# Splitting three of layer two's output-weight pairs earlier, in a two-layer gated network after channel attention

## The chip, the cores and the metric

One core of one Trainium2 chip runs the kernel. The metric is the device time of one execution in microseconds. Three runs of the kernel before took 1188.28, 1188.49 and 1191.84 us; the median is 1188.49.

## The reference

Channel attention over 6016 tokens and 256 channels gives x; two gated layers with 1536 hidden features follow, the first with an RMS norm and silu, the second with a sigmoid:

```python
def _attn_ref(q, k, v, tau):
    qn = q / (np.linalg.norm(q, axis=1, keepdims=True) + 1e-06)
    kn = k / (np.linalg.norm(k, axis=1, keepdims=True) + 1e-06)
    s = kn.transpose(0, 2, 1) @ qn / tau
    a = np.exp(s - s.max(-1, keepdims=True))
    a /= a.sum(-1, keepdims=True) + 1e-09
    return v @ a

def _moe_ref(x, w_gate, w_val, w_out, rms_g):
    rms = np.sqrt(np.mean(x * x, axis=-1, keepdims=True) + 1e-06)
    xn = x / rms * rms_g
    g = xn @ w_gate
    silu = g * (1.0 / (1.0 + np.exp(-g)))
    return silu * (xn @ w_val) @ w_out

def _moe2_ref(x, w_gate, w_val, w_out):
    gate = 1.0 / (1.0 + np.exp(-(x @ w_gate)))
    return gate * (x @ w_val) @ w_out
```

## The kernel before

Every float32 matrix product is made from three matmuls: each operand is split into a high part (a copy on ACT that rounds to float32r) and a low part (a subtraction on DVE), and high x high, high x low and low x high are added up in PSUM (`mm3`, lines 107 to 109). On top of that, pairs of token blocks are multiplied by Strassen's scheme in Winograd's form, with seven products in place of eight.

The order of the work is written out by hand (`manual_schedule`); each engine takes its instructions in that order and stops at the first that has to wait. After the attention and some plain blocks of layer one, the program runs through *periods*. A period takes one of the 12 feature tiles f of one pair of token blocks p through the gate and value products.
- **The old-way block** (`period`, line 731): 12 periods, pair 2 of layer one. The gate and value products have seven factors, the output product is the ordinary one. A period is 33 matmul calls of 448 columns on PE, and 6.68 us long when nothing disturbs it.
- **The joint passes** (`team_period`, line 802): nine passes of 12 periods, three for layer one and six for layer two. Here the output product too has seven factors: six hidden tiles make a team of three pairs, and the team's 21 output products run in the six periods that follow. Accumulating transfers on POOL's queue (line 592) form the sums of hidden tiles.

Between two steps of a period there are named points (`early`, `ACT`, `DVE`, `end`) at which a list of callables is run: `slots[k][point]` belongs to the k-th of the periods still to come.

The joint passes need the *output weights* (w_out) in pairs of feature tiles, split into seven or eight pieces. Each layer has six such pairs. The split of one pair goes in two halves, from the rd buffers in DRAM into the od buffers:
- `out_load` (line 539) loads the four unsplit 128x128 pieces into tile t (256 KB).
- First half: `out_high` (line 547) copies t to its high part h on ACT; `out_low` (line 550) subtracts to the low part on DVE; each is stored to od by one transfer of 256 KB (line 554). `out_sums` (lines 558 to 561) then makes the four Winograd sums in t, on POOL.
- Second half: the same copy, subtraction and two stores, for the sums. It writes the same two tiles for the parts, so it has to wait until the first half's stores have landed.

Layer one's pairs use the tiles t1 to t3 of a pool with one buffer each; layer two's use three tiles of the `yo` ring, which the sums of the token pairs (line 407) use too. Pair i of layer one is split in the old-way block at the ends of periods 2i and 2i + 1. Pair 2u of layer two is split at the ends of periods 10 and 11 of joint pass u + 1, pair 2u + 1 at the ends of periods 0 and 1 of the pass after it. All loads and stores of this go through SP's queue, in the order written, together with the stores and loads of the input weights (gd, gw) and the loads of split output weights (ow, line 605). The input weights of feature tile f lie in the tiles wh`f` and wl`f`; the old-way block is the last to use them, and from there on the joint passes borrow these places.

Of the kernel before, what the change touches and what calls it, by code (L numbers as in the profile page):

```python
# [25 lines left out]
def kernel(  # L26
# [510 lines left out]
    odd = {}  # L537

    def out_load(l, i):
        if l:  # L540
            odd["t"], odd["h"], odd["l"] = (ip3.tile([P, 512], F32, tag="yo", name="o") for _ in range(3))
        else:
            odd["t"], odd["h"], odd["l"] = (sp.tile([P, 512], F32, tag=f"t{u}", name="o") for u in range(1, 4))
        nc.sync.dma_start(out=odd["t"], in_=rd[l][i].rearrange("p u n -> p (u n)"))

    def out_high(l, i):
        nc.scalar.copy(odd["h"].bitcast(F32R), odd["t"])

    def out_low(l, i, first):
        nc.vector.tensor_sub(odd["l"].bitcast(F32R), odd["t"], odd["h"])  # L550
        g, j = divmod(i, NJ)
        for e, t in enumerate((odd["h"], odd["l"])):
            dst = od[l][g][:, first : first + 4, e, j]
            nc.sync.dma_start(out=dst, in_=t.rearrange("p (u n) -> p u n", u=4))

    def out_sums(l, i):
        w11, w21, w12, w22 = (odd["t"][:, u * P : (u + 1) * P] for u in range(4))
# [42 lines left out]
    def ow_load():  # L600
        i, k = divmod(ow_n[0], len(KINDS))
        if i < len(teams):
            tag = ("wh3", "wl3", "wh4", "wl4")[ow_n[0] % 4]
# [299 lines left out]
    with tc.manual_schedule():  # L903
# [255 lines left out]

        def out_weights(l, i, one, two):  # L1160
            for slot, first in ((one, 0), (two, 4)):
                steps = [partial(out_high, l, i), partial(out_low, l, i, first)]
                slot.setdefault("end", []).extend(steps if first else [*steps, partial(out_sums, l, i)])
# [4 lines left out]

        out_load(0, 0)
        pv = None  # L1170
        outs = [(0, b // 2, b % 2, f) for b, f in items[-SKEW:]]
        for n, it in enumerate([*stream, None]):
# [17 lines left out]
            if n < NF and f % 2 == 0:  # L1190
                out_weights(0, f // 2, slots[0], slots[1])
                if f < NF - 2:
                    slots[1]["end"].append(partial(out_load, 0, f // 2 + 1))
            if 0 < n // NF < 4 and f == NF - 3:
                u = 2 * (n // NF - 1)
                slots[0].setdefault("end", []).append(partial(out_load, 1, u))
                out_weights(1, u, slots[1], slots[2])
                slots[2]["end"].append(partial(out_load, 1, u + 1))
            if 1 < n // NF < 5 and f == 0:
                out_weights(1, 2 * (n // NF - 1) - 1, slots[0], slots[1])  # L1200
# [9 lines left out]
            if pv and pv["it"][:2] == (0, PLAIN):  # L1210
# [3 lines left out]
                if g == 6:  # L1214
                    for _ in range(4):
                        ow_load()
# [43 lines left out]
```

## Time and profile before

| | us |
|---|---|
| median of three runs | 1188.49 (1188.28 to 1191.84) |
| the profiled execution | 1191.87 |
| its span, first to last instruction | 1190.1 |
| PE busy (matmuls) | 1156.2, 97% |
| DVE busy | 970.6, 82% |
| ACT busy | 889.9, 75% |
| POOL busy | 342.6, 29% |

PE is the matmul engine, DVE the vector engine, ACT the scalar engine, POOL the GpSimd engine, SP the engine that issues most transfers. All times in the rows are microseconds from the start of the span. A bracket at the end of a row tells how long the engine had been idle before it, and what ended that. In the names, o is any tile of the split above, hh and hl are the parts of a hidden tile, g and v PSUM banks. The old-way block runs from about 313 to 396 us, the joint passes from there to the end.

### The profile page before, as it was taken

How to read it: one execution, taken by the hardware profiler on the slowest of the kernel's cores; microseconds unless marked ns; L12 is line 12 of the kernel's file. 1: busy time of each engine (PE TensorE's matmuls, PEld its weight loads, DVE VectorE, ACT ScalarE, POOL GpSimd, SP SyncE). 2: the span in 40 equal slices, each digit the busy share in tenths (PEclk: the TensorE clock that was granted, in tenths of full speed). 3: DMA queues.
4: the chain of work that ended last, by engine and by line, in shares of the span. 5: the costliest groups of instructions: out<-in, count | busy, mean ns of one | idle time of the engine just before them, and what ended most of it. 6: DMA issues, size and time to landing. Idle time of an engine off the chain costs nothing.

```text
span 1190.1 us, 16698 instructions
## 1 busy us (share of the span) xinstructions
PE 1156.2 (97%) x5236; PEld 961.0 (81%) x5236; DVE 970.6 (82%) x1496; ACT 889.9 (75%) x1663; POOL 342.6 (29%) x399
## 2 busy tenths in 40 slices
PE   8899999999999999999999999999999999999997
PEld 7788788788899778788788778888888888888895
DVE  6798999986567588788898897887888888888877
ACT  6665778765577588787777877887787787787784
POOL 0042777742321122412412411321311321321121
PEclk9899999999999999999999999999999999999999
DMA  9663446774478879999999998998998998998995
GB/s 321 243 217 136 140 143 201 278 248 168 153 264 303 290 220 268 312 260 275 304 272 281 298 276 247 293 258 242 288 265 241 290 263 248 292 261 246 282 253 142
DMA packets 143000, 297.07 MB, mean 250 GB/s; under 512 B 13888, under 2 KB 53312, under 8 KB 142912
## 3 DMA queue, kind: packets, MB, share of 16 engines
q1 hardware_dynamic: 122032, 258.65, 64.3%
q0 software_dynamic: 20736, 37.23, 17.9%
q8 instruction: 41, 0.67, 0.2%
q14 instruction: 47, 0.39, 0.1%
q10 hardware_dynamic: 144, 0.13, 0.0%
HBM read 201.98 MB, written 56.75 MB: 217 GB/s over the span
## 4 chain that ended last, share of the span: by engine, by line
PE 67%; DMA 5%; DVE 3%; issue 3%; ACT 2%; POOL 0%; DVEq 0%; SPq 0%; ACTq 0%; POOLq 0%
PE g L107 10%; PE g L108 10%; PE g L109 10%; PE v L107 5%; PE v L109 5%; PE v L108 5%; PE y L108 4%; PE y L109 4%; PE y L107 4%; PE at L107 4%; PE at L108 4%; PE at L109 4%; DMA od<-o 3%; DMA hs<-hs 1%; DVE hl L648 1%
## 5 line engine op out<-in xcount | busy, mean ns | idle before, releaser
L592 POOL DMA_DIRECT2D hs<-hs x144 | 125.8, 926 | 572.2 <-DVE hl L648 416.3
L648 DVE TENSOR_TENSOR hl<-hs,hh 128x512 fp32r<-128x512 f32 (+1 forms) x324 | 223.8, 702 | 26.3 <-ACT hh L640 25.3
L640 ACT CAST hh<-hs 128x512 fp32r<-128x512 f32 (+1 forms) x324 | 195.0, 613 | 24.6 <-PE at L109 7.3
L833 ACT COPY v<-g 128x512 f32<-128x512 f32 (+1 forms) x210 | 119.0, 567 | 65.2 <-PE g L109 61.9
L838 DVE TENSOR_TENSOR hs<-g,e 128x512 f32<-128x512 f32 (+1 forms) x105 | 71.5, 681 | 67.4 <-ACT v L833 66.7
L107 PE MATMUL g<-xh,gw 128*128 128x512 f32 x240 | 95.0, 396 | 4.1 <-ACT v L833 2.8
L108 PE MATMUL g<-xl,gw 128*128 128x512 f32 x240 | 93.7, 391 | 0.0
L109 PE MATMUL g<-xh,gw 128*128 128x512 f32 x240 | 93.7, 390 | 0.0
L867 ACT ACTIVATE g<-g 128x512 f32<-128x512 f32 (+1 forms) x108 | 67.5, 625 | 29.8 <-DVE g L871 28.9
L108 PE MATMUL y<-hl,ow 128*128 128x512 f32 (+1 forms) x216 | 84.3, 390 | 1.8 <-DVE hl L648 1.7
L107 PE MATMUL y<-hh,ow 128*128 128x512 f32 (+1 forms) x216 | 84.2, 390 | 1.2 <-ACT hh L640 1.2
L109 PE MATMUL y<-hh,ow 128*128 128x512 f32 (+1 forms) x216 | 84.0, 389 | 0.0
L833 ACT COPY g<-g 128x512 f32<-128x512 f32 (+1 forms) x105 | 61.3, 583 | 25.4 <-PE g L109 25.0
L871 DVE TENSOR_TENSOR g<-g,g 128x512 f32<-128x512 f32 (+1 forms) x105 | 70.3, 670 | 5.6 <-PE g L109 5.6
L842 ACT ACTIVATE sg<-v 128x512 f32<-128x512 f32 (+1 forms) x108 | 64.2, 595 | 8.0 <-PE v L109 0.4
L107 PE MATMUL g<-qh,gw 128*128 128x512 f32 (+1 forms) x171 | 66.8, 390 | 2.9 <-ACT v L833 2.1
L108 PE MATMUL g<-ql,gw 128*128 128x512 f32 (+1 forms) x171 | 65.8, 385 | 0.0
L109 PE MATMUL g<-qh,gw 128*128 128x512 f32 (+1 forms) x171 | 65.7, 384 | 0.0
L108 PE MATMUL at<-hl,ow 128*128 128x512 f32 (+1 forms) x162 | 63.5, 392 | 0.5 <-DVE hl L648 0.4
L107 PE MATMUL at<-hh,ow 128*128 128x512 f32 (+1 forms) x162 | 63.2, 390 | 0.1
L109 PE MATMUL at<-hh,ow 128*128 128x512 f32 (+1 forms) x162 | 63.1, 389 | 0.0
L833 ACT COPY e<-g 128x512 f32<-128x512 f32 (+1 forms) x105 | 61.3, 583 | 0.4
(245 smaller groups left out, 3337.3 us busy)
## 6 DMA issues: line engine op xcount, KB each, us to landing
gw<-gd SPq DMA_DIRECT2D x216, 448.0 KB, 5.6
ow<-od SPq DMA_DIRECT2D x126, 384.0 KB, 5.2
hs<-hs POOLq DMA_DIRECT2D x128, 256.0 KB, 7.8
wraw<-in_w_dram SPq DMA_DIRECT2D x24, 768.0 KB, 4.7
od<-o SPq DMA_DIRECT2D x48, 256.0 KB, 4.8
vraw<-in_v_t_dram SPq DMA_DIRECT2D x11, 512.0 KB, 4.8
gd<-w2h SPq DMA_DIRECT2D x12, 448.0 KB, 2.7
gd<-w2l SPq DMA_DIRECT2D x12, 448.0 KB, 3.4
```

Of the source, the lines that this page charges most:

```text
L107: nc.tensor.matmul(ps, sh, mh, start=start, stop=False, skip_group_check=more)
L108: nc.tensor.matmul(ps, sh, ml, start=False, stop=False, skip_group_check=more)
L109: nc.tensor.matmul(ps, sl, mh, start=False, stop=stop, skip_group_check=more)
L592: nc.gpsimd.dma_start(out=to, in_=t, accum_op=ALU.add)
L640: nc.scalar.copy(h, src)
L648: nc.vector.tensor_sub(lo, src, f32(h))
L833: nc.scalar.copy(new(name, make, *args), s[src])
L838: nc.vector.tensor_add(s["v1"], s["Z"], s["e5"])
L842: nc.scalar.activation(out=new("sg0", lambda: t), in_=s["A"], func=acts[l])
L867: "gate": lambda: nc.scalar.activation(out=pv["g1"], in_=pv["g1"], func=acts[pl]),
L871: "g1": lambda: nc.vector.tensor_add(s["g1"], s["g1"], s["B"]),
```

## The change

Three of layer two's six pairs (0 to 2) move from the joint passes into the old-way block: pair j is split at the ends of periods 6 + 2j and 7 + 2j, beside layer one's pair j + 3. Their tiles lie in the places wh3, wl3, wh4 and wl4, five half-tiles for each pair: t, and a high and a low tile for each half, so that the second half waits for no store. The other three pairs (3 to 5) stay in the joint passes, with their first half at the end of period 10 and the second at the end of period 1 of the next pass; both halves still share their two tiles. Layer one's pairs 2 to 5 get a place of their own for t (wh1, wl1, wh5, wl5); the tiles of the parts are shared as before. The table `early` gives the period at whose end a pair is loaded. The first four ow loads, which use wh3 to wl4 too, go from the end of old-way period 7 to the ends of the second and third joint period, two at each.

```diff
--- before.py
+++ after.py
@@ -535,26 +535,36 @@
         mm3(ps[:, :w], ch[:, a], cl[:, a], h[:, :w], lo[:, :w], start, stop, not start)
 
     odd = {}
+    lent_out = ("wh3", "wl3", "wh4", "wl4")
+    lent_in = {2: "wh1", 3: "wl1", 4: "wh5", 5: "wl5"}
 
     def out_load(l, i):
-        if l:
-            odd["t"], odd["h"], odd["l"] = (ip3.tile([P, 512], F32, tag="yo", name="o") for _ in range(3))
+        if l and i < NJ:
+            w = [wp.tile([P, 2, 512], F32, tag=lent_out[(NJ * i + u) % 4], name="o") for u in range(3)]
+            o = [w[u // 2][:, u % 2] for u in range(5)]
         else:
-            odd["t"], odd["h"], odd["l"] = (sp.tile([P, 512], F32, tag=f"t{u}", name="o") for u in range(1, 4))
-        nc.sync.dma_start(out=odd["t"], in_=rd[l][i].rearrange("p u n -> p (u n)"))
-
-    def out_high(l, i):
-        nc.scalar.copy(odd["h"].bitcast(F32R), odd["t"])
+            if l:
+                o = [ip3.tile([P, 512], F32, tag="yo", name="o") for _ in range(3)]
+            else:
+                o = [wp.tile([P, 512], F32, tag=lent_in[i], name="o") if i in lent_in else sp.tile([P, 512], F32, tag="t1", name="o")]
+                o += [sp.tile([P, 512], F32, tag=f"t{u}", name="o") for u in (2, 3)]
+            o += o[1:]
+        odd[l, i] = {"t": o[0], 0: o[1:3], 4: o[3:]}
+        nc.sync.dma_start(out=o[0], in_=rd[l][i].rearrange("p u n -> p (u n)"))
+
+    def out_high(l, i, first):
+        nc.scalar.copy(odd[l, i][first][0].bitcast(F32R), odd[l, i]["t"])
 
     def out_low(l, i, first):
-        nc.vector.tensor_sub(odd["l"].bitcast(F32R), odd["t"], odd["h"])
+        h, lo = odd[l, i][first]
+        nc.vector.tensor_sub(lo.bitcast(F32R), odd[l, i]["t"], h)
         g, j = divmod(i, NJ)
-        for e, t in enumerate((odd["h"], odd["l"])):
+        for e, t in enumerate((h, lo)):
             dst = od[l][g][:, first : first + 4, e, j]
             nc.sync.dma_start(out=dst, in_=t.rearrange("p (u n) -> p u n", u=4))
 
     def out_sums(l, i):
-        w11, w21, w12, w22 = (odd["t"][:, u * P : (u + 1) * P] for u in range(4))
+        w11, w21, w12, w22 = (odd[l, i]["t"][:, u * P : (u + 1) * P] for u in range(4))
         nc.gpsimd.tensor_add(w22, w21, w22)
         nc.gpsimd.tensor_sub(w21, w11, w21)
         nc.gpsimd.tensor_sub(w11, w22, w11)
@@ -600,7 +610,7 @@
     def ow_load():
         i, k = divmod(ow_n[0], len(KINDS))
         if i < len(teams):
-            tag = ("wh3", "wl3", "wh4", "wl4")[ow_n[0] % 4]
+            tag = lent_out[ow_n[0] % 4]
             t = wp.tile([P, 2, NJ, P], F32R, tag=tag, name="ow")
             nc.sync.dma_start(out=f32(t), in_=od[teams[i][0]][teams[i][2]][:, PLACE.index(KINDS[k])])
             ow.append(t)
@@ -1157,15 +1167,19 @@
                     pair_high(*first, i)
                     pair_low(*first, i)
 
+        def halves(l, i, first):
+            steps = [partial(out_high, l, i, first), partial(out_low, l, i, first)]
+            return steps if first else [*steps, partial(out_sums, l, i)]
+
         def out_weights(l, i, one, two):
             for slot, first in ((one, 0), (two, 4)):
-                steps = [partial(out_high, l, i), partial(out_low, l, i, first)]
-                slot.setdefault("end", []).extend(steps if first else [*steps, partial(out_sums, l, i)])
+                slot.setdefault("end", []).extend(halves(l, i, first))
 
         def store_w(f):
             for e, t in enumerate((wh[0, f], wl[0, f])):
                 nc.sync.dma_start(out=gd[0][f][:, e], in_=f32(t[:, :NG]))
 
+        early = {3: [(0, 2)], 4: [(0, 3)], 5: [(1, 0)], 6: [(1, 1)], 7: [(0, 4)], 8: [(0, 5), (1, 2)]}
         out_load(0, 0)
         pv = None
         outs = [(0, b // 2, b % 2, f) for b, f in items[-SKEW:]]
@@ -1187,17 +1201,21 @@
                         slots[3 + i].setdefault("ACT", []).append(partial(pair_high, *nxt, x))
                         slots[4 + i].setdefault("DVE", []).append(partial(pair_low, *nxt, x))
             f = n % NF
-            if n < NF and f % 2 == 0:
-                out_weights(0, f // 2, slots[0], slots[1])
-                if f < NF - 2:
-                    slots[1]["end"].append(partial(out_load, 0, f // 2 + 1))
+            if n < NF:
+                for l, i in early.get(f, ()):
+                    slots[0].setdefault("end", []).append(partial(out_load, l, i))
+                if f % 2 == 0:
+                    out_weights(0, f // 2, slots[0], slots[1])
+                if f in (6, 8, 10):
+                    out_weights(1, f // 2 - 3, slots[0], slots[1])
+                if f == 0:
+                    slots[1]["end"].append(partial(out_load, 0, 1))
             if 0 < n // NF < 4 and f == NF - 3:
-                u = 2 * (n // NF - 1)
+                u = n // NF + 2
                 slots[0].setdefault("end", []).append(partial(out_load, 1, u))
-                out_weights(1, u, slots[1], slots[2])
-                slots[2]["end"].append(partial(out_load, 1, u + 1))
+                slots[1].setdefault("end", []).extend(halves(1, u, 0))
             if 1 < n // NF < 5 and f == 0:
-                out_weights(1, 2 * (n // NF - 1) - 1, slots[0], slots[1])
+                slots[1].setdefault("end", []).extend(halves(1, n // NF + 1, 4))
             if n == 0:
                 for f in range(NF):
                     slots[f].setdefault("end", []).append(partial(store_w, f))
@@ -1211,9 +1229,9 @@
                 g = pv["it"][2]
                 if 6 < g < 10:
                     gw_load(g - 7)
-                if g == 6:
-                    for _ in range(4):
-                        ow_load()
+            if n in (NF + 1, NF + 2):
+                ow_load()
+                ow_load()
             pv = s
             outs = [(*it[:2], e, it[2]) for e in (1, 0)] if n < len(alone) else []
 
```

Three places show what it moves. ACT at the head of joint pass 2, from the end of period 0 to that of period 1; before (hh is a high part of a hidden tile, v<-g and e<-g the copies out of PSUM, o the copy of a half):

```order
L547 CAST o<-o 128x512
L640 CAST hh<-t 128x512
L867 ACTIVATE g_5019<-g_5019 128x512
L640 CAST hh<-hs 128x512
L833 COPY v<-g 128x512
L640 CAST hh<-hs 128x512
L833 COPY e_5120<-g 128x512
L833 COPY g_5134<-g 128x512
L842 ACTIVATE sg<-v 128x512
L640 CAST hh<-hs 128x512
L833 COPY v<-g 128x512
L547 CAST o<-o 128x512
```

The same stretch now:

```order
L650 CAST hh<-t 128x512 x2
L877 ACTIVATE g_5059<-g_5059 128x512
L650 CAST hh<-hs 128x512
L843 COPY v<-g 128x512
L650 CAST hh<-hs 128x512
L843 COPY e_5152<-g 128x512
L843 COPY g_5166<-g 128x512
L852 ACTIVATE sg<-v 128x512
L650 CAST hh<-hs 128x512
L843 COPY v<-g 128x512
L556 CAST o<-o 128x512
```

The copy of the first half is gone from period 0 (it stands in period 10 of the pass before); that of the second half stands in the same place as before.

ACT at the end of old-way period 9 before, from a token pair's high part (line 375) to the copy of the next period's first bank:

```order
L375 CAST qh<-xs 128x512
L774 COPY v<-g 128x448
L547 CAST o<-o 128x512
L750 ACTIVATE g_3921<-g_3921 128x448
L752 COPY v<-g 128x448
```

The same place now:

```order
L375 CAST qh<-xs 128x512
L784 COPY v<-g 128x448
L556 CAST o<-o 128x512 x2
L760 ACTIVATE g_3933<-g_3933 128x448
L762 COPY v<-g 128x448
```

Two casts stand where one stood, layer one's and then layer two's; so it is at the ends of periods 6 to 11, and on DVE with the subtractions.

SP's queue around the ends of old-way periods 7 and 8 before (rd_133 and rd_134 hold layer one's unsplit pairs 4 and 5, rd_137 layer two's pair 2; od_142 takes layer one's split pairs, od_143 layer two's):

```order
L554 DMA od_142<-o 128x4x128 x2
L544 DMA o<-rd_133 128x512
L605 DMA ow<-od_141 128x768 x4
L1167 DMA gd_113<-wh 128x896
L1167 DMA gd_113<-wl 128x896
L554 DMA od_142<-o 128x4x128 x2
L527 DMA gw<-gd_105 128x896 x2
```

The same place now:

```order
L564 DMA od_142<-o 128x4x128 x2
L564 DMA od_143<-o 128x4x128 x2
L553 DMA o<-rd_133 128x512
L1180 DMA gd_113<-wh 128x896
L1180 DMA gd_113<-wl 128x896
L553 DMA o<-rd_134 128x512
L553 DMA o<-rd_137 128x512
L564 DMA od_142<-o 128x4x128 x2
L564 DMA od_143<-o 128x4x128 x2
L527 DMA gw<-gd_105 128x896 x2
```

Two more stores stand at each end, the four ow loads are gone, and the load of pair 5 (rd_134), which stood behind the stores of period 9, stands ahead of those of period 8.

## Rows read from the trace of the kernel before

**Rows 1.** The page, its first line.

```profile
span 1190.1 us, 16698 instructions
```

**Rows 2.** Joint passes 2 to 5: stretch, length, busy us by engine, clock, DMA share, GB/s.

```profile
477.19:567.63 90.44, 88.23 (x380) 71.79 (x379) 75.49 (x120) 70.45 (x131) 24.89 (x29) 0.98 0.97 283
567.63:658.78 91.15, 88.34 (x386) 71.71 (x385) 77.50 (x121) 71.94 (x131) 26.43 (x31) 1.00 0.98 284
658.78:746.76 87.98, 86.11 (x374) 69.20 (x373) 74.28 (x116) 69.63 (x128) 21.39 (x23) 1.00 0.94 272
746.76:832.81 86.05, 86.01 (x380) 70.85 (x379) 72.75 (x116) 68.69 (x126) 19.11 (x20) 1.00 0.93 267
```

**Rows 3.** The list of waits: who waits for whom, us in total, times, longest.

```profile
ACT o L547 <- DMA od<-o: 9.6, 4, 3.6
```

**Rows 4.** Timeline at the head of pass 2: start, us, engine, line, operation, [idle before].

```profile
479.88 0.37 SPq L554 DMA_DIRECT2D od<-o  x1
...
490.14 0.62 ACT L547 CAST o<-o 128x512 fp32r<-128x512 f32 x1 [3.58 <-DMA od<-o]
...
492.35 0.50 PE L107 MATMUL g<-xh,gw 128*128 128x512 f32 x1 [2.21 <-ACT v L833]
```

**Rows 5.** Timeline at the heads of passes 3 and 4.

```profile
580.49 0.62 ACT L547 CAST o<-o 128x512 fp32r<-128x512 f32 x1 [3.49 <-DMA od<-o]
...
657.49 1.28 ACT L842 ACT_TABLE_LOAD   x1
...
670.08 0.62 ACT L547 CAST o<-o 128x512 fp32r<-128x512 f32 x1 [1.92 <-DMA od<-o]
```

**Rows 6.** Transfers issued at 360:363, 381:383, 479.5:482: median us to landing (last).

```profile
od<-o SPq DMA_DIRECT2D x2, 256.0 KB, 2.2
...
od<-o SPq DMA_DIRECT2D x2, 256.0 KB, 6.5
...
od<-o SPq DMA_DIRECT2D x2, 256.0 KB, 10.2
```

**Rows 7.** By stretches, as rows 2: behind the stop in pass 2.

```profile
493.53:496.94 3.41, 3.41 (x10) 2.66 (x9) 1.10 (x2) 1.00 (x2) 3.31 (x4) 0.50 1.08 377
```

**Rows 8.** Timeline, old-way periods 9 and 10.

```profile
380.49 0.62 ACT L547 CAST o<-o 128x512 fp32r<-128x512 f32 x1 [0.64 <-DMA od<-o]
...
389.46 0.62 ACT L547 CAST o<-o 128x512 fp32r<-128x512 f32 x1 [2.93 <-DMA o<-rd]
...
391.04 0.47 PE L107 MATMUL g<-xh,wh 128*128 128x448 f32 x1 [1.47 <-ACT v L752]
```

**Rows 9.** Timeline, end of old-way period 7 and what follows.

```profile
366.38 0.62 ACT L547 CAST o<-o 128x512 fp32r<-128x512 f32 x1
...
367.57 0.69 DVE L550 TENSOR_TENSOR o<-o 128x512 fp32r<-128x512 f32 x1
367.69 0.58 ACT L750 ACTIVATE g<-g 128x448 f32<-128x448 f32 x1 [0.68 <-DVE g L778]
...
368.30 0.63 DVE L751 TENSOR_TENSOR v<-v,g 128x448 f32<-128x448 f32 x1
...
369.56 0.63 DVE L728 TENSOR_TENSOR hl<-v,hh 128x448 fp32r<-128x448 f32 x1 [0.63 <-ACT hh L727]
...
370.76 0.36 PE L108 MATMUL at<-hl,wh 128*128 128x448 f32 x1
```

**Rows 10.** Timeline of POOL: first and last of a pair's four sums.

```profile
361.70 0.86 POOL L558 TENSOR_TENSOR o<-o 128x128 f32<-128x128 f32 x1 [10.63 <-DVE o L550]
...
363.98 0.46 POOL L561 TENSOR_TENSOR o<-o 128x128 f32<-128x128 f32 x1
```

**Rows 11.** By stretches, as rows 2: one calm and three full old-way periods.

```profile
359.76:366.44 6.68, 6.68 (x35) 6.19 (x34) 4.86 (x8) 5.16 (x12) 2.51 (x4) 1.00 0.65 238
373.13:393.18 20.05, 18.58 (x91) 16.56 (x90) 13.21 (x22) 12.85 (x26) 4.52 (x8) 1.00 1.05 371
```

**Rows 12.** Timeline of DVE while POOL makes a pair's sums.

```profile
648.23 0.95 DVE L572 SCALAR_TENSOR_TENSOR hs<-hs,g 128x512 f32<-128x512 f32 x1
```

## The prediction

> **What bounds the kernel now.** I read the page first: PE is busy for 97% of a span of 1190.1 us [rows 1], so a change that leaves PE's 33 matmuls of an old-way period and its product lists alone can only move the time by PE's idle stretches. Which stage has them is read from a table by stretches, cut at the first gate of each joint pass (the ScalarE activation of line 842). A pass that splits no output weights takes 86.05 us with PE busy for 86.01. The three passes that have a pair in their first two periods take 90.44, 91.15 and 87.98 [rows 2]: 4.39, 5.10 and 1.93 more, 11.42 together. The list of waits names the reason: ACT's copy of line 547 (a half's high part) waits for the landing of an od store four times, 9.6 us in all [rows 3].
>
> The timeline shows the mechanism. In pass 2 the first half of pair 1 sends its od stores at 479.88, at the end of period 0; the second half, one period later, writes the same two tiles, so the copy of line 547 stands idle for 3.58 us until 490.14. Behind it in ACT's queue are the gate and the copy of line 833, and PE waits for that copy 2.21 us [rows 4]. The same stands at 580.49 (3.49 us) and at 670.08 (1.92 us) [rows 5]. An od store lands 2.2 us after its issue in a calm old-way period, 6.5 in a full one, 10.2 at the head of a pass [rows 6]; a half follows its partner by about 7 us, so only the last is far too late. After the stop in pass 2 PE ran for 3.41 us at a granted clock of 0.50, which is 1.2 GHz instead of 2.4 [rows 7]. It had idled 2.21 us before; the stops of the other two passes show no such fall.
>
> **The joint passes after the change.** Three of the six pairs of layer two are gone from here. The other three have their first half at the end of period 10 and their second at the end of period 1 of the next pass, 21 us apart, and the stores land in at most 10.2. So no od wait is left. What stays of the 11.42 us:
> - The activation table load of 1.28 us at 657.49 [rows 5], where the gate changes from silu to sigmoid. It stays in full: 1.28.
> - Five halves inside these stretches (periods 1 and 10 of two passes, period 1 of the third). Such a half without a wait holds ACT for 0.62 [rows 4] and DVE for 0.69 [rows 9]. It costs PE between nothing, in a gap, and 0.62 on the path; ACT and DVE have gaps but few, and I take 0.25: 1.25 together, bounds 0 and 3.1.
>
> Saved: 11.42 - 1.28 - 1.25 = 8.9 us, bounds 7.0 and 10.1. Of it the half clock is about 1.4: ten matmuls stand in the 3.41 us, which at the 0.226 us of a calm pass (86.05 for 380) would be 2.26, so 1.15 is lost; half of 3.41, or 1.7, is the most; I take the middle. The pair sums on POOL at the end of period 2 wait for the same stores as before and get them no later, and SP loses four stores and a load at each head, so nothing new waits there.
>
> **The old-way block.** Here the work grows: in periods 6 to 11 two halves stand where one stood.
> - ACT: in a calm period the cast of line 547 starts at 366.38, and ACT then idles for 0.68 until the gate at 367.69, waiting for DVE [rows 9]. Two casts of 0.62 end at 367.62: the second fits, with 0.07 to spare. Nothing; what it costs without that cover is its 0.62.
> - DVE: the second subtraction comes before the multiply of line 751. The first starts at 367.57, the multiply at 368.30 [rows 9]; two subtractions of 0.69 put it at 368.95, 0.65 late. The hl that hangs on it ended at 370.19 and ends at 370.84 then; PE wants it at 370.76 [rows 9], so it is 0.08 late. From 0 to 0.65 a period; I take the 0.1 that the rows give: 0.6 for six periods.
> - POOL: the four sums of one pair take from 361.70 to 364.44 [rows 10]. Two pairs end at 367.2, and the second cast of the next period wants them at 367.00 (366.38 and 0.62). ACT is 0.2 late, less the 0.07 to spare: 0.15 in three periods, 0.45; 0 to 0.9.
> - The wait that goes: layer one's last pair was loaded late, ACT waited 2.93 us for it at 389.46, and PE idled 1.47 [rows 8]. Its tile is now its own and the load starts a period sooner. Saved: 1.5.
> - DMA, the doubtful term. Layer one's halves still share one pair of tiles for the parts, so each waits for the store of the half before, which has about 6.0 us to land. In the stretch of periods 9 to 11 the engines were full (share 1.05) and moved 371 GB/s, 2.48 MB in 6.68 us [rows 11]. Period 8 now moves four od stores, two gw and two gd transfers and two loads, 3.41 MB; periods 9 and 10 move 2.89 each. Behind after two of these: 1.34 MB, 3.6 us; another 1.0 us I take over from period 7, where two more stores and a load (0.79 MB, 2.1 us) come at a period's end and the free third of a period [rows 11] takes up about half of them. With the calm landing of 2.2 [rows 6] that is 6.8 us against 6.0. I take 1.0 us of PE's time for the last waits; the bounds are 0, and 6 if reads behind writes slow the queue by another fifth. Now the slack of 0.68 on ACT, which swallowed a wait of 0.64 at 380.49 [rows 8], is used up. The four ow loads (1.57 MB) leave period 7 for the second and third joint period, four periods before the first is used.
>
> Old-way block: -1.5 + 0.6 + 0.45 + 1.0 = 0.55 longer, bounds 1.5 shorter and 6 longer.
>
> **The sum.** The profiled execution took 1191.87 us, 1.8 around its span. 1191.87 - 8.9 + 0.55 = 1183.5. The median of the runs is 1188.49, 3.4 below the profiled run. A fall of the clock as in rows 7 would be 1.4 of the difference, and I take it that the median run has none there: so 7.5 is saved instead of 8.9, and 1188.49 - 7.5 + 0.55 = 1181.5 us.
>
> **Rivals.**
> 1. The old-way block is free: the stores land in time and DVE's halves fall into gaps. For it: shares of 0.65 in a period before the gw loads [rows 11]. Then only the 1.5 saved counts, and the five joint halves cost little too: 1188.49 - (10.1 - 1.4) - 1.5 = 1178.3.
> 2. DMA binds the end of the old-way block: the upper bound of 6 us. For it: 6.5 us to landing already, with half the od stores [rows 6]. Against it: the late load was the wait that cost there, not a store. 1188.49 - 7.5 + 6 = 1187.0: no change that can be told.
> 3. POOL and DVE slow each other. A DVE line of about 0.68 took 0.95 beside POOL's sums at 648.23 [rows 12], 0.27 more. Twelve more POOL sums stand in the block; if each costs one DVE step 0.27 on PE's path, 3.2 us: 1184.7. The Trainium skill has the stronger form (page "SBUF — State Buffer", section "Who interferes with whom"): a VectorE instruction with two SBUF inputs and a GpSimd instruction that reads SBUF exclude each other for a whole instruction. The trace agrees that they disturb each other, at 0.27 us rather than a whole sum. By that rule twelve sums of 0.46 to 0.86 us would block 7.5 us, and the gain would be gone: 1189.0. The sum above stands without it.
> 4. Slower: ACT's queue in periods 8 to 11, where layer one's copy now waits with no slack behind it. If od landings reach the 10.2 us that the heads of the passes have, each of the four copies waits as those did and PE loses 2.21 and a half-clock stretch of 1.4, 14.4 together: 1188.49 - 7.5 - 1.5 + 14.4 = 1193.9. It decides from a landing of about 8.5 us on. Against it: POOL's accumulating transfers, which fill the engines at the heads (line 592) run only in the joint passes.
>
> **How the numbers follow.** Forecast 55% (1179.5 to 1185.5 its own range), rival 1 20%, rival 2 12%, rival 3 7%, rival 4 6%. A measurement of this kernel can tell about 0.3%, 3.6 us, from no change: faster is below 1184.9. The forecast lies below it nine times in ten, rival 1 always, rival 3 half the time, rival 2 one time in five: 0.50 + 0.20 + 0.035 + 0.025, or 0.76; slower is rival 4 and a trace of 2 and 3, 0.07; the same, 0.17. The range of 8 in 10 leaves out rival 4 and the lowest part of rival 1: 1177.5 to 1188.0.
>
> **What would show it.** Right: the three pass lengths at 86.5, 87.8 and 86.3; no wait of line 556 for od in any pass; PE without an idle of over 0.3 us at the heads; in the old-way block no wait for an o load, waits for od of about 1 us at its very end. Wrong: a copy of line 556 idle for over 2 us in periods 8 to 11, a subtraction of line 560 ahead of a late hl with PE waiting for it in every period, or passes that stay at 90 us with another releaser.

## The result, and the profile after

The changed kernel took 1177.24 us, the median of four runs (1174.98 to 1181.23), against 1188.38 of four runs of the kernel before on the same chip (1186.82 to 1191.84): a ratio of 0.9909, interval 0.9889 to 0.9929. The forecast was 1181.5, its range 1177.5 to 1188.0: faster, as forecast, and 0.3 us below the low end. A later set of runs gave 1181.12 against 1188.75, a ratio of 0.993 (0.9918 to 0.9943); the size is taken up below.

The profiled execution took 1177.59 us. The page's first line answers to [rows 1]:

```profile
span 1175.8 us, 16704 instructions
```

The span is 14.3 us shorter. Cut at the first gates, as the prediction cuts it, the difference lies here (us):

| stretch | before | after | difference | forecast |
|---|---|---|---|---|
| up to the first gate of the old-way block | 316.18 | 310.95 | -5.23 | 0 |
| old-way block | 85.86 | 86.00 | +0.14 | +0.55 |
| pass 1 | 75.15 | 75.14 | -0.01 | 0 |
| passes 2 to 4 | 269.57 | 260.68 | -8.89 | -8.9 |
| pass 5 to the end | 443.3 | 443.0 | -0.3 | 0 |

The first row lies ahead of anything the change touches. In the twelve other profiles of this study that gate stands between 309.6 and 314.6 us, for the kernel before at 310.1: it is scatter of what lies ahead of the block, and no part of the change. Passes 2 to 5 by stretches, with the columns of [rows 2]:

```profile
472.09:559.02 86.93, 86.26 (x380) 70.76 (x379) 74.96 (x118) 69.65 (x128) 22.32 (x25) 1.00 0.96 278
559.02:647.26 88.24, 87.66 (x386) 71.95 (x385) 75.65 (x119) 71.06 (x129) 23.37 (x27) 1.00 0.97 281
647.26:732.77 85.51, 85.23 (x374) 69.44 (x373) 72.60 (x115) 69.20 (x126) 18.45 (x19) 1.00 0.93 266
732.77:818.77 86.00, 85.97 (x380) 70.83 (x379) 72.72 (x116) 68.65 (x126) 19.06 (x20) 1.00 0.93 267
```

Pass 5, which had no split before, has its old length; the clock is full in all four. In the list of waits one line is left of what [rows 3] showed, and it belongs to the old-way block:

```profile
ACT o L556 <- DMA od<-o: 0.6, 1, 0.6
```

At the head of pass 2, ACT in the timeline, where [rows 4] had 3.58 us:

```profile
480.61 0.57 ACT L843 COPY v<-g 128x512 f32<-128x512 f32 x1
481.09 0.62 ACT L556 CAST o<-o 128x512 fp32r<-128x512 f32 x1
...
483.38 0.57 ACT L843 COPY v<-g 128x512 f32<-128x512 f32 x1 [0.22 <-PE g L109]
```

The copy of the half follows at once, and the next copy of line 843 waits for PE, not PE for it. What is left at the heads is shorter and comes two periods later, in period 3: PE waits for DVE there (line 848), 0.67 us in pass 2, and 0.58 and 0.24 in passes 3 and 4.

```profile
497.56 0.50 PE L107 MATMUL g<-xh,gw 128*128 128x512 f32 x1 [0.67 <-DVE hs L848]
```

The end of the old-way block, where [rows 8] had the late load:

```profile
383.14 1.15 ACT L556 CAST o<-o 128x512 fp32r<-128x512 f32 x2
...
390.74 1.14 ACT L556 CAST o<-o 128x512 fp32r<-128x512 f32 x2 [0.61 <-DMA od<-o]
```

The od stores issued from 383 to 392 us land as follows (least, median, most), beside 6.5 in [rows 6]:

```profile
DMA to landing us min/median/max: 5.0/6.6/7.0
```

DVE, POOL and PE at the end of period 6, and DVE at the end of period 7, to be read against [rows 9, 10]:

```profile
356.39 1.29 DVE L560 TENSOR_TENSOR o<-o 128x512 fp32r<-128x512 f32 x2
357.21 0.79 POOL L568 TENSOR_TENSOR o<-o 128x128 f32<-128x128 f32 x1 [10.90 <-PE g L109]
357.59 0.89 DVE L761 TENSOR_TENSOR v<-v,g 128x448 f32<-128x448 f32 x1
359.11 0.71 DVE L738 TENSOR_TENSOR hl<-v,hh 128x448 fp32r<-128x448 f32 x1 [0.63 <-ACT hh L737]
...
359.48 0.37 PE L107 MATMUL at<-hh,wh 128*128 128x448 f32 x1
359.88 0.47 PE L108 MATMUL at<-hl,wh 128*128 128x448 f32 x1
...
363.48 1.29 DVE L560 TENSOR_TENSOR o<-o 128x512 fp32r<-128x512 f32 x2
364.68 0.62 DVE L761 TENSOR_TENSOR v<-v,g 128x448 f32<-128x448 f32 x1
```

At the end of an even period DVE's multiply (line 761) takes 0.89 us beside POOL's first sum, and PE starts on hl 0.40 us after the matmul before it, where the usual step is 0.20; the next step takes 0.31, so some 0.3 us are lost. In the second profile of this kernel the two steps are 0.49 and 0.31, 0.4 lost. At the end of an odd period, which has the same two subtractions and no sums, the multiply takes 0.62 and PE loses nothing.

### The profile page after: what moved, and what is told of

Same layout as the page of the kernel before. It is cut to its first block, busy times and chain, and to the rows that moved or that the text cites. A ratio compares the mean times of both kernels' runs of the same rounds, so it can differ in the third digit from the quotient of the medians.

```text
span 1175.8 us, 16704 instructions
## 1 busy us (share of the span) xinstructions
PE 1150.5 (98%) x5236; PEld 957.4 (81%) x5236; DVE 969.7 (82%) x1496; ACT 889.8 (76%) x1663; POOL 340.3 (29%) x399
## 4 chain that ended last, share of the span: by engine, by line
PE 71%; DVE 4%; issue 3%; DMA 2%; ACT 1%; POOL 0%; DVEq 0%; ACTq 0%; SPq 0%; POOLq 0%
PE g L107 11%; PE g L109 11%; PE g L108 11%; PE v L107 5%; PE v L108 5%; PE v L109 5%; PE y L109 4%; PE y L107 4%; PE y L108 4%; PE at L107 4%; PE at L108 4%; PE at L109 4%; DVE hl L658 1%; DMA od<-o 1%; DMA hs<-hs 1%
```

## The experiments

**Both kernels profiled once more.** No edit; one run with a profile of each.

> The kernel before, once more, unchanged, for a second profile. The two profiles so far differ by 14.3 us of span, of which 5.2 lie ahead of the old-way block, where the change touches nothing. Theory: this is scatter of the first 50 us (input loads and a stretch of half clock at 43 us), so the start of the old-way block moves by some us between executions of one kernel, while passes 2, 3 and 4 again take about 90.4, 91.2 and 88.0 us and the old-way block 85.9. Rival: the head is slower in this kernel in every execution, first gate copy of the old-way block at 316 us again, and then the change touches the head in some way.

> The changed kernel, once more, unchanged, for a second profile. Theory: passes 2, 3 and 4 again at 86.9, 88.2 and 85.5 us; matmuls of 448 columns in the old-way block came every 207 ns in the first profile of it against 203 before, which I take for a passing state of the engine: here 203, and the block then about 1 us shorter than 86.0. Rival: the pitch of 207 belongs to the changed kernel and comes again in the whole block.

Single runs of 1185.14 and 1177.5 us. Passes 2 to 4 together, the sum rows of the table by stretches, before and after:

```profile
sum 269.08, PE 262.61 PEld 212.69 DVE 227.05 ACT 212.08 POOL 72.69; mean PE 87.53 PEld 70.89 DVE 75.68 ACT 70.69 POOL 24.23
```

```profile
sum 260.56, PE 259.25 PEld 212.14 DVE 222.96 ACT 209.88 POOL 64.19; mean PE 86.42 PEld 70.71 DVE 74.32 ACT 69.96 POOL 21.40
```

The passes are 8.5 us shorter, the old-way block 85.45 and 85.82. The kernel before stops PE at the head of pass 2 and falls to half clock again (timeline, then the stretch behind it):

```profile
485.61 0.79 PE L107 MATMUL g<-xh,gw 128*128 128x512 f32 x1 [1.97 <-ACT v L833]
```

```profile
485.60:488.80 3.20, 3.19 (x8) 2.52 (x9) 2.22 (x4) 1.80 (x4) 3.06 (x4) 0.50 1.08 382
```

**Is it the wait?** The kernel before with the second halves of pairs 1, 3 and 5 moved from the end of period 1 to the point `ACT` of period 2; all else, the six pairs in the joint passes too, as before.

```diff
-                out_weights(1, 2 * (n // NF - 1) - 1, slots[0], slots[1])
+                i = 2 * (n // NF - 1) - 1
+                slots[0].setdefault("end", []).extend(
+                    [partial(out_high, 1, i), partial(out_low, 1, i, 0), partial(out_sums, 1, i)]
+                )
+                slots[2].setdefault("ACT", []).extend([partial(out_high, 1, i), partial(out_low, 1, i, 4)])
```

> The kernel before with one edit: the second half of pairs 1, 3 and 5 of layer two stands at the ACT point of period 2 and not at the end of period 1, so that the stores of the first half have 4 to 5 us longer to land. All six pairs stay in the joint passes, with the same copies, subtractions, sums and stores. Theory (the wait for the od stores is what the change removes): the idle of 3.58, 3.49 and 1.92 us before the second copy falls below 0.7 us, passes 2 to 4 fall from 90.4, 91.2 and 88.0 to about 87, 88.5 and 86.5, 7.5 us together, ratio to before about 0.9935. Rival (it is the amount of splitting work in the passes that costs): passes stay within 2 us of before, since the work is all still there; ratio over 0.998.

Measured: 1185.18 us, ratio 0.997 (0.9954 to 0.9986); passes 2 to 4 together, and four lines of the timeline:

```profile
sum 265.51, PE 261.93 PEld 211.07 DVE 227.75 ACT 211.74 POOL 72.63; mean PE 87.31 PEld 70.36 DVE 75.92 ACT 70.58 POOL 24.21
```

```profile
490.46 0.62 ACT L547 CAST o<-o 128x512 fp32r<-128x512 f32 x1
...
499.81 1.30 POOL L407 TENSOR_TENSOR xs<-zl,xs 128x512 f32<-128x512 f32 x1 [6.63 <-DMA ow<-od]
...
509.25 0.39 PE L109 MATMUL v<-xh,gw 128*128 128x512 f32 x1
510.56 0.50 PE L107 MATMUL g<-xh,gw 128*128 128x512 f32 x1 [0.93 <-ACT v L833]
```

and in the list of waits:

```profile
POOL xs L407 <- DMA od<-o: 11.1, 2, 6.2
```

ACT's copy waits for nothing, and no stretch at half clock is left in the pass. But only 3.6 of the 8.5 us come. The stores of the late half land at 499.59 and 501.31, and POOL's sums of the token pairs, which take their tiles from the same ring, wait for them (not so in the kernel before). The bracket at 499.81 names an ow load, but POOL's queue goes on 0.03 us after the store of 499.59 has landed, and in passes 3 and 4 the list names the od stores. Behind these sums in POOL's queue stands an accumulating transfer; it lands at 509.31, and ACT's next cast, which needs it, starts at 509.41 after 1.81 us idle. PE stops at 510.56, and at the same place of pass 3. The wait moved from ACT to POOL, which neither theory had; the changed kernel doesn't pay this price.

The two stops make period 4 of passes 2 and 3 8.70 and 8.91 us long in place of 7.48: 2.7 of the 4.9 us that are missing. Most of the rest is in pass 4, 87.54 us against 85.5 in the changed kernel, where no od store holds up ACT and PE waits 0.59 and 0.86 us for DVE. The first of these waits comes in the kernel before too (0.58), and not in the changed kernel, which has no half at the end of period 0: a half there has a price of its own, with or without a wait for a store.

**Does putting it back cost the gain?** The changed kernel with its three remaining pairs back at the ends of periods 0 and 1, in their two shared tiles.

```diff
-                slots[0].setdefault("end", []).append(partial(out_load, 1, u))
-                slots[1].setdefault("end", []).extend(halves(1, u, 0))
+                slots[2].setdefault("end", []).append(partial(out_load, 1, u))
...
-                slots[1].setdefault("end", []).extend(halves(1, n // NF + 1, 4))
+                out_weights(1, n // NF + 1, slots[0], slots[1])
```

> The changed kernel with one part undone: the three pairs that stay in the joint passes are loaded at the end of period 11 and split at the ends of periods 0 and 1, as pairs 1, 3 and 5 were before, with the shared tiles. Half the splitting work is still gone from the passes. Theory (the wait): ACT again idles for 2 to 3.5 us before the second copies, passes 2 to 4 again at about 90, 91 and 88 us, and of the gain little is left: ratio to before 0.997 to 1.0. Rival (the amount of work): the passes stay near those of the changed kernel, 87, 88 and 85.5, ratio 0.991.

Measured: 1184.99 us, ratio 0.998 (0.9965 to 0.9995). The sum over passes 2 to 4, and the stop in pass 2:

```profile
sum 266.07, PE 260.83 PEld 211.62 DVE 224.87 ACT 210.05 POOL 67.21; mean PE 86.94 PEld 70.54 DVE 74.96 ACT 70.02 POOL 22.40
```

```profile
484.63 0.62 ACT L556 CAST o<-o 128x512 fp32r<-128x512 f32 x1 [2.64 <-DMA od<-o]
...
486.84 0.50 PE L107 MATMUL g<-xh,gw 128*128 128x512 f32 x1 [1.31 <-ACT v L843]
```

5.5 of the 8.5 us are lost again by where the two halves stand alone, with three pairs moved away. Most of the gain is the distance between two halves that share tiles, as the first theory had it; the other 3.0 us stay with three pairs gone from the passes. The stop of 1.31 brings no half clock.

**How large is it, and what are the early loads worth?** The changed kernel in five more rounds; and with layer one's pairs 2 to 5 loaded as before, one tile behind the stores of the pair before:

```diff
-                o = [wp.tile([P, 512], F32, tag=lent_in[i], name="o") if i in lent_in else sp.tile([P, 512], F32, tag="t1", name="o")]
+                o = [sp.tile([P, 512], F32, tag="t1", name="o")]
...
-        early = {3: [(0, 2)], 4: [(0, 3)], 5: [(1, 0)], 6: [(1, 1)], 7: [(0, 4)], 8: [(0, 5), (1, 2)]}
+        early = {5: [(1, 0)], 6: [(1, 1)], 8: [(1, 2)]}
...
-                if f == 0:
-                    slots[1]["end"].append(partial(out_load, 0, 1))
+                if f % 2 == 0 and f < NF - 2:
+                    slots[1]["end"].append(partial(out_load, 0, f // 2 + 1))
```

> The changed kernel once more, unchanged, with more rounds. Theory: the change is worth what the two traces show stage by stage (about 8.5 us in passes 2 to 4, of it 1.2 to 1.5 a clock fall at the head of pass 2, and 0.1 to 0.4 given back in the old-way block); runs of the two kernels with the same mean granted clock stand about 7 us apart, and the medians 8 to 9: ratio 0.9925 to 0.9935. Rival: the 11 us between the first medians are the change's own; ratio 0.991 or less, and runs of the same clock stand 10 us or more apart.

> The changed kernel, with layer one's pairs 1 to 5 loaded as before, into one tile behind the stores of the pair before. Theory: the early loads are worth the stall that the kernel before has at the end of period 9 (ACT 2.0 to 2.9 us, PE 1.0 to 1.5); with twice the stores ahead of the load the wait is longer still, 3 to 5 us of ACT, and the block is 1.5 to 3.5 us longer than the changed kernel's 85.8: 87.3 to 89.3. Rival: that stall has another cause and the early loads of layer one are worth nothing: 85.8 to 86.2.

The changed kernel: 1181.12 us, ratio 0.993 (0.9918 to 0.9943), as the theory had it. With late loads a single run took 1183.77 us. Timeline and stretches there:

```profile
389.16 1.14 ACT L556 CAST o<-o 128x512 fp32r<-128x512 f32 x2 [3.29 <-DMA o<-rd]
...
391.26 0.52 PE L107 MATMUL g<-xh,wh 128*128 128x448 f32 x1 [2.28 <-ACT v L762]
```

```profile
391.30:394.90 3.60, 3.60 (x10) 3.26 (x11) 2.37 (x4) 2.41 (x5) 3.21 (x7) 0.53 1.08 373
314.58:403.56 88.98, 85.56 (x404) 76.11 (x402) 59.83 (x99) 62.65 (x124) 27.23 (x40) 0.98 0.89 297
```

The block is 88.98 us, 1.7 to 3.2 longer than in three profiles of the changed kernel (87.31, 86.00, 85.82): a stop of 2.28 us, with 3.6 us at about half clock behind it. That is what the tile of its own is worth by this one run; without it the block would have eaten a fifth to over a third of the gain.

**What holds PE up at the ends of even periods?** The changed kernel without POOL's sums of the three moved pairs, and then without layer one's either:

```diff
-            return steps if first else [*steps, partial(out_sums, l, i)]
+            return steps if first or (l and i < NJ) else [*steps, partial(out_sums, l, i)]
```

```diff
-            return steps if first else [*steps, partial(out_sums, l, i)]
+            return steps if first or (l and i < NJ) or (not l and i >= NJ) else [*steps, partial(out_sums, l, i)]
```

> The changed kernel without POOL's sums for the three pairs that were moved (their second halves split the unsummed pieces, so this part of the computation is left out). Theory: the stalls of 0.4 us of PE for hl after periods 6, 8 and 10 of the old-way block come from DVE working beside POOL's sums of two pairs; they vanish, and the block is 1.2 us shorter (84.6 in place of 85.8). Rival: they come from the second subtraction on DVE alone; they stay at 0.4 and the block at 85.8.

> The changed kernel without POOL's sums for layer two's pairs 0 to 2 and for layer one's pairs 3 to 5 (their second halves split the unsummed pieces, so this part of the computation is left out): POOL makes no sum at the ends of periods 6, 8 and 10 of the old-way block. Theory: the second subtraction pushes DVE's multiply of line 761 into the first of layer one's sums, where it takes 0.88 us in place of 0.63; without any sum it takes 0.63, and the stalls of 0.39 us of PE for hl near 360 and 374 vanish, as there are none at the ends of periods 7 and 9, which have the second subtraction and no sums. Rival: the second subtraction alone makes hl late; the stalls stay at 0.3 to 0.4.

Without the moved pairs' sums the stall stays (1176.21 us, one run; end of period 6 in the timeline):

```profile
356.11 0.88 DVE L761 TENSOR_TENSOR v<-v,g 128x448 f32<-128x448 f32 x1
...
357.89 0.36 PE L107 MATMUL at<-hh,wh 128*128 128x448 f32 x1
358.39 0.47 PE L108 MATMUL at<-hl,wh 128*128 128x448 f32 x1
```

Without any sums it is gone (1179.63 us, one run):

```profile
359.81 0.62 DVE L761 TENSOR_TENSOR v<-v,g 128x448 f32<-128x448 f32 x1
...
361.60 0.37 PE L107 MATMUL at<-hh,wh 128*128 128x448 f32 x1
361.80 0.41 PE L108 MATMUL at<-hl,wh 128*128 128x448 f32 x1
```

The block is 85.12 us then, against 85.82, 86.00 and 87.31 in three profiles of the changed kernel. The first of the two experiments refuted my theory as I put it (that it takes the sums of two pairs); the second settles it: the second subtraction pushes the multiply into the sums that were there before, layer one's. In the kernel before the multiply started 0.09 us ahead of the first sum and took 0.63; it was the sum that took longer, 0.86 us [rows 10] where one alone takes 0.46:

```profile
361.61 0.63 DVE L751 TENSOR_TENSOR v<-v,g 128x448 f32<-128x448 f32 x1
```

**Can the rest be had?** The changed kernel with the second halves of pairs 3 to 5 at the end of period 11, where the stores of period 10 are 7 us old; run twice:

```diff
-                slots[1].setdefault("end", []).extend(halves(1, u, 0))
-            if 1 < n // NF < 5 and f == 0:
-                slots[1].setdefault("end", []).extend(halves(1, n // NF + 1, 4))
+                out_weights(1, u, slots[1], slots[2])
```

> The changed kernel, with the second half of the three remaining pairs at the end of period 11, one period behind the first, in place of period 1 of the next pass. Theory: what is left at the heads is DVE's backlog from that half's subtraction (PE late by 0.83, 0.74 and 0.40 near 496, 583 and 671 us); it goes, and the stores of period 10 land in 5.5 us, 7.2 us ahead of the half that needs their tiles, so no new wait comes: passes 2 to 4 together 1.0 to 1.5 us shorter than in the changed kernel (259.1 to 259.6 in place of 260.6). Rival: the half costs the same wherever it stands, or waits for its stores in period 11 as it did at the heads: 260.5 or more.

> The changed kernel with the second halves of pairs 3 to 5 at the end of period 11, once more beside the run above, so that the two stand on the same chip. Theory: ratio 0.992, as it was; passes 2 to 4 together 259.3 us.

Ratios 0.992 (0.9906 to 0.9933) and 0.9897 (0.9882 to 0.9913), medians 1179.55 and 1177.14. Passes 2 to 4 take 259.28 us in the first and 259.26 in the second, 1.1 to 1.4 less than in the three profiles of the changed kernel, as forecast:

```profile
sum 259.28, PE 259.19 PEld 212.13 DVE 221.64 ACT 209.30 POOL 63.04; mean PE 86.40 PEld 70.71 DVE 73.88 ACT 69.77 POOL 21.01
```

On top of that, the first halves of pairs 0 to 2 at a later point of the old-way period, and then layer one's last half one period later:

```diff
-                    out_weights(1, f // 2 - 3, slots[0], slots[1])
+                    slots[1].setdefault("early", []).extend(halves(1, f // 2 - 3, 0))
+                    slots[1].setdefault("end", []).extend(halves(1, f // 2 - 3, 4))
```

```diff
-                if f % 2 == 0:
+                if f % 2 == 0 and f < NF - 2:
                     out_weights(0, f // 2, slots[0], slots[1])
+                if f == NF - 2:
+                    slots[0].setdefault("end", []).extend(halves(0, NJ + 2, 0))
...
+            if n == NF:
+                slots[0].setdefault("end", []).extend(halves(0, NJ + 2, 4))
```

> The kernel with the second halves of pairs 3 to 5 at the end of period 11, and in the old-way block the first halves of pairs 0 to 2 not at the ends of periods 6, 8 and 10 but 2 us later, at the point ahead of the second bank's copy in the next period (DVE's multiply then comes first, and POOL's sums begin behind it as in the kernel before). Theory: the stalls for hl near 360 and 374 vanish, and the stores of these halves no longer stand beside layer one's: the old-way block is 0.8 to 1.5 us shorter (84.8 to 85.5 in place of 86.3), the ratio 0.990 to 0.992. Rival: ACT's cast there delays the copy that PE waits for, so that the cost only moves: block 86.0 or more, ratio 0.992 or more.

> The kernel of the run before (second halves of pairs 3 to 5 at the end of period 11, first halves of pairs 0 to 2 at the later point), and the second half of layer one's last pair moved from the end of old-way period 11 to the end of the first joint period, one period behind. Theory: the last wait for an od store at the end of the old-way block (2.1 us of ACT near 395, which makes period 11 9.6 us in place of 8.4) goes; the block is 1.0 us shorter than that kernel's 87.0, and the ratio stands 0.001 below that of the kernel with the second halves at the end of period 11 alone. Rival: ACT and DVE are full in the first joint periods, which have no output products on PE to cover them, so the half costs its 0.6 to 1.3 us there and the two kernels can't be told apart.

Ratios 0.9905 (0.988 to 0.993) and 0.9903 (0.9885 to 0.9921): neither can be told from the version above. In the first the stalls for hl near 361 and 375 are gone, but the block is longer, 87.03 us. About 0.9 us of it is the longer step of the matmuls that the last section describes; more comes from its last od wait, which makes period 11 9.62 us long:

```profile
394.98 1.14 ACT L556 CAST o<-o 128x512 fp32r<-128x512 f32 x2 [2.13 <-DMA od<-o]
```

In the second the block is short and pass 1 long; block and pass 1 there, and in the second run of the version with the halves at the end of period 11 alone:

```profile
311.62:396.51 84.89, 83.73 (x404) 74.91 (x402) 59.94 (x98) 61.76 (x122) 26.43 (x40) 1.00 0.87 297
396.51:472.81 76.30, 75.48 (x323) 59.84 (x324) 59.57 (x93) 59.87 (x112) 17.81 (x19) 1.00 0.93 283
```

```profile
311.24:397.05 85.81, 84.27 (x404) 74.79 (x402) 60.40 (x99) 62.62 (x123) 27.09 (x40) 1.00 0.87 298
397.05:472.25 75.20, 75.08 (x323) 59.92 (x324) 59.02 (x92) 59.28 (x112) 17.78 (x19) 1.00 0.93 283
```

161.19 and 161.01 us together: the two can't be told apart, as the rival had it. The late half makes PE wait 0.62 us for ACT in period 1 of pass 1 (at 403.14), as the rival said. What it saves hangs on the landing before it: period 11 is 8.38 us long, 1.2 less than in the run before, but no less than in the run shown beside it. Another 0.5 us of pass 1 stands in period 3, behind a load of input weights, and came in the run before too, with no half there. The version with the second halves at the end of period 11 alone is as good and the simplest, and by its passes some 1.3 us better than the changed kernel.

## Why the prediction was right, and where it was not

**The passes.** The term of 8.9 us is what the profiles show: 8.89, and 8.5 in the second pair of profiles. That no od wait would be left came true. Pass by pass it was 86.9, 88.2 and 85.5, for 86.5, 87.8 and 86.3 forecast, and PE idles over 0.3 us at two of the three heads, where the forecast had it below. Inside what stays the shares were otherwise. The table load was put at 1.28; period 11 of pass 3, which ends with it, is 8.55 us long against 7.14 in a clean pass, but the period behind it is 6.44 against 7.14, so 0.7 stays. The five halves were put at 0.25 each; the two in period 10 cost 0.25 (7.73 against 7.48), the three in period 1 about 0.4, as moving them showed: the subtraction puts DVE behind, and PE waits for it in period 3. The two errors cancel, which is luck: 2.6 us stay over 3 x 86.0, where the forecast had 2.53.

**The step that failed: "I take it that the median run has none there".** With it I took 1.4 us for half clock off the median's gain. But the kernel before fell to half clock at the head of pass 2 in both profiles, and none of the twelve profiles of the other kernels fell there (the longest stop at that place was 1.31 us). The 54 runs of the kernel before in the four later sets have a median of 1188.1 us and a mean granted clock of 0.9933, the ten of the changed kernel 1178.55 and 0.9950. The missing share of the clock, 0.0017 of 1188 us, is 2.0 us. Of the 9.5 us between these medians 2.0 are thus, by estimate, the clock's and 7.5 the waits', for which the forecast's terms have 7.5 - 0.55, or 7.0. At equal clock the kernels stand as far apart: 6.8 us at 0.994 (13 runs and 2), 7.8 at 0.995 (8 and 3). The four runs of the changed kernel in the first set, 11.1 us below those of before, had a mean clock of 0.9960; the five of the second, 7.6 below, 0.9942. These sums mix several chips. Side by side on one chip the clock's share is smaller: 1.4 of the 7.6 us of the second set (0.9942 against 0.9930), and the kernel with the late second halves ("Is it the wait?"), which has no fall there, had 0.9942 against 0.9940 of the kernel before. So the fall is shown in two profiles; in how many of the other runs it comes is not shown. Why the clock falls elsewhere, in the attention stage and in the last pass of most profiles, stays open.

**The old-way block.** Forecast 0.55 longer; measured 0.14 and 0.4 in the two pairs. Its single profiles scatter more than that: 85.86 and 85.45 before, 86.00, 85.82 and 87.31 after. Cut down to the changed periods 6 to 11 they are 44.24 and 43.28 before, and 42.99 in the kernel with the late second halves, which has the same block; and 43.57 to 44.60, mean 44.0, in six profiles with the changed block: 0.3 to 0.5 longer. By steps:
- ACT's second cast free: right; behind it the gate still waited 0.17 and 0.16 for DVE in the two profiles.
- DVE's second subtraction, 0.1 a period: wrong in its spread. Nothing at odd ends, 0.3 to 0.4 at even ones, 1.0 to 1.2 in all in place of 0.6.
- POOL's two chains of sums making ACT late, 0.45: wrong, no cast waited for a sum. The cost of POOL was another, to stretch DVE's multiply.
- The late load, 1.5 saved: right in kind, but no fixed size. Behind it PE stopped 1.47 and 0.50 us in the two profiles of the kernel before, and not at all in the kernel with the late second halves, where ACT waited 0.96. By the undone part 1.5 is an underestimate; with the doubled stores ahead of it the load would have cost 1.7 to 3.2. A wait of 0.38 us for an o load came in the second profile of the changed kernel, where the forecast had none.
- The last od waits, 1.0: ACT waited 0.6, 0.3 and 1.6 us in three profiles; landing 6.6 in the first, at most 7.0, against the 6.8 worked out.

**The rivals.** Rival 1 (a free block) and 2 (six us of DMA) did not come. That 1177.24 lies nearer to rival 1's 1178.3 than to the forecast is chance: the block did not get shorter, and the four runs had a high clock. Rival 4 needed landings of 8.5 us; none over 7.3 came at the end of the block in three profiles of the changed kernel.

Rival 3 had the mechanism of the even ends, and the prediction read its own row of it wrongly. It took 0.27 us [rows 12] as a price, less than a whole sum. The delay is what is left of POOL's instruction when DVE's starts, less 0.13 to 0.15 us. So it is in all 278 cases, in the fourteen profiles from the old-way block on, in which a DVE instruction with both inputs in SBUF starts with a third of a us or more left of a sum or difference on POOL; those with an input in PSUM lose nothing beside the same POOL instructions (the 106 of hs<-g,e, for one). The multiply at 357.59 had 0.41 left and lost 0.27, as did rows 12. The kernel before has a longer case, 1.21 left and 1.07 lost:

```profile
416.64 1.30 POOL L407 TENSOR_TENSOR xs<-xl 128x512 f32<-128x512 f32 x1
416.73 1.76 DVE L572 SCALAR_TENSOR_TENSOR hs<-hs,g 128x512 f32<-128x512 f32 x1 [0.54 <-ACT g L867]
```

The form that I cited (the Trainium skill, "SBUF — State Buffer", "Who interferes with whom") has the two exclude each other, and the order of issue decide who waits; the trace agrees, with 0.27 us lost by the multiply that comes second and none by the one that comes first. The later one waits for the rest of one sum, so neither the 0.27 a sum nor the 7.5 us for twelve was the right price. Only the multiply that the second subtraction displaced meets a sum on PE's path, three times and not twelve.

## What to carry to other kernels

Two stages that reuse one buffer through a store want a distance longer than the landing of that store under load, not in a calm stretch: space them, or give each its own tile, before thinking of doing less. Price a stall with the clock fall that a trace shows behind it, and don't take it that the median run goes without: here both profiles had it. And when an instruction is put in a gap of one engine, look at what the displaced instruction now runs beside, and which of the two starts first: 0.65 us of delay was free, until it moved a multiply from just ahead of the neighbour's sums to just behind the start of one.

## What was not expected of the hardware

Stops of 2.21, 1.97 and 2.28 us were followed by half clock; stops of 2.12 and 1.83 at the head of pass 3 were not (the first of them in the same execution as the 2.21). The length of the stop alone doesn't decide it.

The 448-column matmuls of the old-way block stand at one of two steps. In the changed kernel's profile (five steps from the first line to the second):

```profile
358.24 0.37 PE L107 MATMUL g<-xh,wh 128*128 128x448 f32 x1
...
359.27 0.37 PE L109 MATMUL v<-xh,wl 128*128 128x448 f32 x1
```

and without any sums:

```profile
363.06 0.36 PE L108 MATMUL g<-xl,wh 128*128 128x448 f32 x1
...
364.07 0.36 PE L107 MATMUL y<-hh,wh 128*128 128x448 f32 x1
```

That is 0.206 and 0.202 us each, at a granted clock of 1.00 in both. Eight of the twelve periods ran at the longer step in the changed kernel's profile, hardly one in the second profile of the same kernel, none in the two of the kernel before, and eight in that of the kernel with the late second halves, which has the old block; 33 matmuls of a period make 0.13 us of it, about 1 us of the block. Which of the two a run gets, and why, is open; it is part of the block's scatter.
